# The expert guess of six batches by a sum over the partitions on GpSimd, and two w2 conversions at other hidden blocks

## The chip, the cores and the metric

The kernel runs on one core of a Trainium2 chip. The metric is the device time of one execution in microseconds (us); less is better. Times of the trace count from the start of the profiled span.

## The reference

Two stages: packed attention over 8 batches of 8 heads (576 tokens, 64 wide, 32 packing rows), then a mixture of 8 experts with one expert for each token.

```
p_packed = softmax(p @ k.T / 8) @ v           # per batch and head
out      = softmax(q @ p_packed.T / 8) @ p_packed
x        = out as [4608, 512]                  # 576 tokens of each batch
logits   = normed(x) @ normed(expert_emb).T / tau
expert   = argmax(logits); gate = the softmax's value there
out[t]   = gate[t] * (relu(x[t] @ w1[expert]) @ w2[expert])
```

All tensors are float32.

## The kernel before

The kernel works batch by batch and joins two batches at a time in one hand-made order: while TensorE runs the expert network (`ffn`) of batch b, the attention of batch b+1 is woven in, one piece at each step of `ffn`. `step_att` advances the generator `att_main(b + 1)`, `gates_main` that of the gates; every `yield` is a place where the other generators may put work. The order in which the generators call the engines is the order of each engine's queue, and an engine takes its queue in order.

Since all tokens of a batch are expected to go to one expert, the kernel **guesses** the expert from the packed rows before the tokens are routed. `row_logits` makes 16 logits for each of 128 packed rows on TensorE, `logits_out` (L521) copies them into `x.ppx`, and `guess` sums them over the 128 partitions by a product with ones (`equal`, L629, into PSUM). VectorE takes the largest of eight columns (L635 to L640), and the index is loaded into a register (L644) with which `load_w1` (L933) and `load_w2` (L941) fetch that expert's weights. For batches 2 to 7 GpSimd loads the register and issues these transfers. At the end the number of tokens that went elsewhere is counted, and a slow loop follows if it isn't zero.

`ffn` of a batch has these stages on TensorE: 16 hidden blocks of six products (`hidden`, L1046; f = 0 to 7 for the first half of the tokens, then for the second), each evicted by ScalarE and VectorE (hT, L1050 and L1051); 16 steps' worth of small products L1081; then four output blocks c = 0 to 3 with w2 (L1099). PSUM has three banks for these results (`pf`).

w2 comes as float32 (`w2r`) and is **converted** in eight pieces into a high and a low part (`split_w2`): a cast on ScalarE (L951) and a subtraction on GpSimd (L952). Four of a batch's eight are made during c = 3 of the batch before, four at f = 4 to 7 of the second half of its own hidden blocks.

Of the attention of the next batch these pieces matter here, in the order in which they come: the **key maxima** of both head groups together on VectorE (L343, `quarter_max`, and `whole_max` behind them); the exponentials on ScalarE (L364); `quarter_flip`, which adds the exponentials together by three halvings for each group on GpSimd (L383, into qs) and transposes them on VectorE (L386); the products with the values on TensorE (L396), and right behind them `quarter_totals`, four small products that read qs (L407), and the count of the batch before (L879). Then the logits and the guess, the query scores (L270), the softmax of the queries (L675 on) up to the transposed `x.at`, which `route` multiplies on TensorE (L764).

Of the kernel before, what the change touches and what calls it, by code (L numbers as in the profile page):

```python
# [9 lines left out]
F32 = mybir.dt.float32  # L10
# [4 lines left out]
ALU = mybir.AluOpType  # L15
AX = mybir.AxisListType
# [11 lines left out]
def kernel(  # L28
# [12 lines left out]
    nc = tc.nc  # L41
    B, H, S, D = q.shape
    E, DM, F = w1.shape
    NP = p.shape[2]
    NG = H // HB
# [207 lines left out]
    def idle(n):  # L253
        for _ in range(n):
            yield
# [264 lines left out]
    def logits_out(x, pt):  # L520
        nc.vector.tensor_copy(x.ppx[:, :, 2 * D :], pt[:, : NG * E].rearrange("p (g e) -> p g e", g=NG))  # L521
# [6 lines left out]
    def att1(x, nat, queries=None, other=None):  # L528

        def pack(queries, other):  # L530
            pack_tiles(x)
            if not x.s1:
                quarter_banks(x)
            quarter_scores(x)
            yield
            for g in range(NG):
                quarter_max(x, g)
            yield
            yield from whole_max(x)
            yield from idle(2)  # L540
            for g in range(NG):
                for n in range(HB):
                    quarter_exp(x, g, n)
                    if n:
                        yield
                quarter_flip(x, g)
            yield
            pt = pb.tile([P, 1024], F32, name="pt", tag="pb")
            for g in range(NG):
                quarter_values(x, g, nat(2 * NPR + g), pt[:, g * D : g * D + D])  # L550
            sums = pt[:, NG * D : NG * D + NG * QW // 8]
            quarter_totals(x, sums)
            if other:
                counts(other, pt[:1, 256 : 256 + NC5 * E])
            next(queries)
            yield
            if other:
                counted(other)
            quarter_sums(x, sums.rearrange("p (g k) -> p g k", g=NG))
            for g in range(NG):  # L560
                pair_rows(x, g, pt[:, g * D : g * D + D])
            yield
            next(queries)
            yield
            pu = pc.tile([P, 512], F32, name="pu", tag="pu")
            for g in range(NG):
                pair_turn(x, g, pu)
            nc.vector.tensor_copy(x.T, pu[:, 0 : NG * P])
            yield from idle(2)
            pt = pc.tile([P, 512], F32, name="pu", tag="pu")  # L570
            row_logits(x, pt)
            yield
            logits_out(x, pt)
            next(queries)
            yield

        def pack_slowly():
            pack_tiles(x)
            for g in range(NG):
                pt = pb.tile([P, 1024], F32, name="pt", tag="pb")  # L580
                p1_turn(x, g, pt)
                yield
                p1_evac(x, g, pt)
                key_sum(x, g)
                yield
            pt = pb.tile([P, 1024], F32, name="pt", tag="pb")
            for g in range(NG):
                pack_values(x, g, nat(2 * NPR + g), pt[:, g * D : g * D + D])
            yield
            for g in range(NG):  # L590
                pair_rows(x, g, pt[:, g * D : g * D + D])
            yield
            pu = pc.tile([P, 512], F32, name="pu", tag="pu")
            yield
            for g in range(NG):
                pair_turn(x, g, pu)
            yield
            nc.vector.tensor_copy(x.T, pu[:, 0 : NG * P])
            yield
            pt = pc.tile([P, 512], F32, name="pu", tag="pu")  # L600
            row_logits(x, pt)
            logits_out(x, pt)
            yield

        if x.halves:
            for g in range(NG):
                key_max(x, g)
                yield
                key_exp(x, g)
                yield  # L610
            yield from pack_slowly()
        else:
            asked = queries or all_queries(x, nat)
            yield from pack(asked, other)
            if queries is None:
                drain(asked)


    def guess(x, late=0, engine=mybir.EngineType.Pool, total=None):
        pt = pc.tile([P, 512], F32, name="pu", tag="pu")  # L620
        if total is not None:

            for n in range(NPR):
                nc.tensor.matmul(
                    pt[:1, :E], total[:, n : n + 1], enT[:, n], start=(n == 0), stop=(n == NPR - 1)
                )
        else:
            for g in range(NG):
                nc.tensor.matmul(  # L629
                    pt[:64, :E], equal, x.ppx[:, g, 2 * D :], start=(g == 0), stop=(g == NG - 1)  # L630
                )
        yield
        m8 = sm.tile([1, 8], F32, name="m8", tag="m8", bufs=1)
        idx = sm.tile([1, 8], U32, name="idx", tag="idx", bufs=1)
        nc.vector.max(m8, pt[:1, :E])  # L635
        nc.vector.max_index(idx, m8, pt[:1, :E])
        gi = sm.tile([1, 1], F32, name="gi", tag="gi", bufs=1)
        nc.vector.tensor_copy(gi, idx[:, 0:1])
        x.sel = sm.tile([1, E], F32, name="sel", tag="sel")
        nc.vector.tensor_scalar(  # L640
            out=x.sel, in0=ecol[:1], scalar1=gi, scalar2=None, op0=ALU.is_equal
        )
        yield from idle(late)
        x.e = nc.values_load(  # L644
            idx[0:1, 0:1], engines=[engine], min_val=0, max_val=E - 1,
            skip_runtime_bounds_check_because="an index of the largest of E columns",
        )


    def att2(x, after=None, first=False, b1=False, eng1="vvvvvv"):  # L650
# [344 lines left out]
    def ffn(x, store, late=False, after=None, end=False, between=None):  # L995
# [33 lines left out]
        def hidden(hf, f):  # L1029
            cs = slice(hf * HS, (hf + 1) * HS)  # L1030
            pf = ps.tile([P, 512], F32, name="pf", tag="pf")

            assert not late or hf == 0 or hf in x.lows and x.gs >= NG * (f // 4 + 1)
            if late and hf == 0:
                ops = [
                    (x.g32[f // 4][:, g, f % 4 * P : f % 4 * P + P], x.ats[0][:, g])
                    for g in range(NG)
                ]
            else:
                ops = [  # L1040
                    (x.G[:, a, g, f * P : (f + 1) * P], x.AT[:, m, g, cs])
                    for g in range(NG)
                    for a, m in PASSES
                ]
            for n, (w, r) in enumerate(ops):
                nc.tensor.matmul(pf[:, :HS], w, r, start=(n == 0), stop=(n == len(ops) - 1))  # L1046
            yield
            n = HS if hf == 0 else 512 - HS
            cs = slice(hf * HS, hf * HS + n)
            nc.scalar.activation(hT[:, 0, f, cs], pf[:, :n], AF.Relu)  # L1050
            nc.vector.scalar_tensor_tensor(  # L1051
                out=hT[:, 1, f, cs], in0=pf[:, :n], scalar=0.0,
                in1=hT[:, 0, f, cs].bitcast(F32), op0=ALU.max, op1=ALU.subtract,
            )
            if hf:
                nc.vector.tensor_scalar(
                    out=h4[:, f], in0=pf[:, n:HS], scalar1=0.0, scalar2=None, op0=ALU.max
                )
            if f >= 4 and hf and not late:
                split_w2(x)  # L1060

        if not late and not hasattr(x, "w1g"):
# [98 lines left out]
    def att_main(b):  # L1161
        x = bat[b]
        if b:
            if b > 1:
                quarter_banks(x)
            queries = all_queries(x, nat_main(b)) if b > 1 else None
            yield from att1(x, nat_main(b), queries, bat[b - 1] if b > 1 else None)
            sync = b == 1
            queue = nc.sync if sync else nc.gpsimd
            for n, _ in enumerate(guess(  # L1170
                x, 0 if sync else 2, mybir.EngineType.SP if sync else mybir.EngineType.Pool
            )):
                if n == 1 and queries:
                    next(queries)
                yield
            load_w1(x, x.e, queue=queue)
        flips = keys_main(b + 1) if b else None
        second = att2(x, flips, b == 0, b < 1, ENG1 if b == 1 else "vvvvpv")
        if b:
            if b > 1:  # L1180
                yield
            for _ in range(3 if b == 1 else 2):
                yield next(second)
            load_w2(x, x.e, queue)
            if b == 1:
                yield from idle(3)
        yield from second
        x.soft = True
        if b:
# [470 lines left out]
```

## Time and profile before

| | |
|---|---|
| median of 3 runs | 417.68 us (417.46 to 417.93) |
| the profiled execution | 418.19 us, its span 416.4 us |
| TensorE (PE) busy | 404.1 us, 97% |
| VectorE (DVE) busy | 304.0 us, 73% |
| ScalarE (ACT) busy | 203.0 us, 49% |
| GpSimd (POOL) busy | 159.2 us, 38% |

The span runs from the first to the last instruction; some 1.8 us of the execution lie around it. From about 81 to 370 us the trace repeats one pattern six times, once for each of the batches 1 to 6 whose `ffn` holds the attention of a later one. A start time of a TensorE product is where it enters the array; its end is modelled.

### The profile page before, as it was taken

To read this page: it belongs to the slowest core of one execution; us is meant where nothing else is said; L and a number is where in the kernel's file an instruction comes from. 1 tells how busy PE (TensorE), PEld (TensorE's weight loads), DVE (VectorE), ACT (ScalarE), POOL (GpSimd) and SP (SyncE) were. 2 spreads that over 40 slices of the span, in tenths; PEclk is the share of its full clock that TensorE was granted. 3 is DMA by queue.
4 is the path that set the end of the run, shared out by engine and by line. 5 is a ranking of instruction groups with operands and counts; after the bars stand their busy time and mean duration, and the time that the engine had idled before them with its cause. 6 is when DMAs were issued, how large, how long until landed. Compare 5 with 4: busy or idle time off the path is not lost.

```text
span 416.4 us, 11127 instructions
## 1 busy us (share of the span) xinstructions
PE 404.1 (97%) x4036; PEld 325.9 (78%) x4037; DVE 304.0 (73%) x968; ACT 203.0 (49%) x501; POOL 159.2 (38%) x197
## 2 busy tenths in 40 slices
PE   6899999999999999999999999999999999999993
PEld 3758768797878978798787978689786988779783
DVE  2577696589986889679896889778896798736500
ACT  3577714863256713764147623666038631576110
POOL 2246714536214571236415381146613373142200
PEclk9999999999999999999999999999999999999998
DMA  8999897976989479876999669995899709310021
GB/s 228 308 347 237 222 293 251 237 188 163 283 309 235 135 209 267 304 211 180 260 344 238 158 177 275 327 229 145 230 305 291 195 23 358 111 51 2 20 53 50
DMA packets 42608, 87.93 MB, mean 211 GB/s; under 512 B 11690, under 2 KB 20906, under 8 KB 42546
## 3 DMA queue, kind: packets, MB, share of 16 engines
q1 hardware_dynamic: 35280, 61.44, 53.0%
q0 software_dynamic: 6720, 25.17, 18.9%
q10 hardware_dynamic: 546, 0.54, 0.6%
q8 instruction: 34, 0.56, 0.6%
q14 instruction: 28, 0.23, 0.2%
HBM read 77.68 MB, written 9.44 MB: 209 GB/s over the span
## 4 chain that ended last, share of the span: by engine, by line
PE 92%; DMA 2%; ACT 1%; DVE 1%; POOL 1%; issue 0%; SPq 0%; ACTq 0%; POOLq 0%
PE pf L1099 43%; PE pf L1046 24%; PE pf L1081 7%; PE pt L764 3%; PE pt L976 3%; PE pt L396 2%; PE pt L270 2%; PE pt L331 2%; DMA nat<-in_k 2%; PE pu L764 1%; PE pf L1243 1%; PE pt L1275 1%; PE pt L464 1%; PE pu L501 0%; DMA out<-o 0%
## 5 line engine op out<-in xcount | busy, mean ns | idle before, releaser
L1099 PE MATMUL pf<-w2s,hT 128*128 128x512 f32 (+1 forms) x792 | 181.8, 387 | 0.0
L1099 PEld LDWEIGHTS pf<-w2s,hT 128*128 128x128 f32 x792 | 143.7, 188 | 39.0 <-issue 10.7
L1046 PE MATMUL pf<-AT,G 128*128 128x288 f32 x720 | 102.1, 298 | 0.4 <-DVE hT L1051 0.2
L1046 PEld LDWEIGHTS pf<-AT,G 128*128 128x128 f32 x720 | 97.2, 188 | 4.3 <-issue 1.5
L952 POOL TENSOR_TENSOR w2s<-w2r,w2s 128x512 fp32r<-128x512 f32 x64 | 81.3, 1288 | 41.2 <-ACT w2s L951 35.7
L1051 DVE SCALAR_TENSOR_TENSOR hT<-pf,hT 128x224 fp32r<-128x224 f32 (+1 forms) x128 | 52.3, 414 | 25.9 <-ACT hT L1050 25.5
L1050 ACT ACTIVATE hT<-pf 128x224 fp32r<-128x224 f32 (+1 forms) x128 | 49.3, 386 | 42.8 <-PE pf L1046 40.1
L291 DVE STREAM_TRANSPOSE kt<-nat 128x576 f32<-128x576 f32 x52 | 38.8, 763 | 0.2
L951 ACT CAST w2s<-w2r 128x512 fp32r<-128x512 f32 x64 | 38.9, 621 | 0.0
L1448 ACT ACTIVATE o<-pf,gate 128x512 f32<-128x512 f32 (+1 forms) x41 | 26.0, 636 | 25.8 <-PE pf L1099 15.5
L1081 PE MATMUL pf<-w2r,h 128*64 128x256 f32 x256 | 33.3, 388 | 0.0
L989 DVE TENSOR_TENSOR G<-pt,G 128x1024 fp32r<-128x1024 f32 x14 | 17.1, 1225 | 20.2 <-ACT G L988 20.2
L715 POOL TENSOR_TENSOR AT<-at,AT 128x576 fp32r<-128x576 f32 x7 | 10.0, 1423 | 53.4 <-ACT AT L710 53.4
L914 ACT ACTIVATE lg<-lg 128x40 f32<-128x40 f32 x8 | 1.9, 237 | 52.9 <-DVE lg L910 52.9
L689 ACT ACTIVATE st<-st 128x576 f32<-128x576 f32 (+1 forms) x17 | 11.1, 657 | 33.9 <-DVE st L686 32.7
L383 POOL TENSOR_TENSOR qs<-p 128x320 f32<-128x320 f32 x12 | 10.5, 879 | 40.6 <-ACT p L364 40.6
L777 ACT ACTIVATE scr<-pt 128x512 f32<-128x512 f32 (+2 forms) x33 | 16.7, 508 | 15.2 <-PE pf L764 7.7
L1081 PEld LDWEIGHTS pf<-w2r,h 128*64 128x64 f32 x256 | 19.4, 137 | 4.9 <-PE pu L501 1.0
L871 POOL MEMSET oh<- 64x8 f32 x8 | 0.8, 98 | 53.8 <-DVE oh L867 48.8
L710 ACT CAST AT<-at 128x576 fp32r<-128x576 f32 x15 | 10.1, 674 | 22.7 <-DVE at L704 22.6
L364 ACT ACTIVATE p<-pt,qnm 128x160 f32<-128x160 f32 x48 | 17.8, 398 | 0.0
L941 POOL DMA_DIRECT2D w2r<-in_moe_w x24 | 17.0, 713 | 0.0
(229 smaller groups left out, 510.2 us busy)
## 6 DMA issues: line engine op xcount, KB each, us to landing
nat<-in_q SPq DMA_DIRECT2D x112, 140.0 KB, 3.4
nat<-in_k SPq DMA_DIRECT2D x96, 140.0 KB, 3.9
w1t<-in_moe_w POOLq DMA_DIRECT2D x12, 1024.0 KB, 9.4
w2r<-in_moe_w POOLq DMA_DIRECT2D x24, 512.0 KB, 15.9
out<-o SPq DMA_DIRECT2D x124, 64.0 KB, 2.4
w2r<-in_moe_w SPq DMA_DIRECT2D x8, 512.0 KB, 9.1
vn<-in_v SPq DMA_DIRECT2D x24, 160.0 KB, 3.7
vn<-in_v SPq DMA_DIRECT2D x48, 80.0 KB, 3.6
```

Of the source, the lines that this page charges most:

```text
L291: nc.vector.transpose(kt.rearrange("p (c i) -> p c i", i=32), t)
L364: nc.scalar.activation(x.p1[g][:, n * QW : n * QW + QW], area(x, g)[:, n // 2, n % 2], AF.Exp, bias=x.nm[:, at : at + 1],)
L941: queue.dma_start(t, w2e[:, 2 * i : 2 * i + 2, :])
L951: nc.scalar.copy(t[:, 0], raw)
L952: nc.gpsimd.tensor_tensor(out=t[:, 1], in0=raw, in1=t[:, 0].bitcast(F32), op=ALU.subtract)
L989: nc.vector.tensor_tensor(out=to[1], in0=src, in1=to[0].bitcast(F32), op=ALU.subtract)
L1046: nc.tensor.matmul(pf[:, :HS], w, r, start=(n == 0), stop=(n == len(ops) - 1))
L1050: nc.scalar.activation(hT[:, 0, f, cs], pf[:, :n], AF.Relu)
L1051: nc.vector.scalar_tensor_tensor(out=hT[:, 1, f, cs], in0=pf[:, :n], scalar=0.0, in1=hT[:, 0, f, cs].bitcast(F32), op0=ALU.max, op1=ALU.su ...
L1081: nc.tensor.matmul(pf[64 * hf : 64 * hf + 64, :256], h4[:, f], x.w2r[f // 2][:, f % 2, hf * 256 : hf * 256 + 256], start=(f == 0), stop=(f ...
L1099: nc.tensor.matmul(pf[:, :w], hT[:, a, f, c * P : (c + 1) * P], x.w2s[f][:, m, at : at + w], start=(f == 0 and i == 0), stop=(f == NF - 1 ...
L1448: nc.scalar.activation(o[:, :w], pf[:, :w], AF.Copy, scale=x.gate[:, c : c + 1])
```

## The change

For batches 2 to 7 the two products L629 go. In their place `vote` puts a `tensor_reduce` over the partitions on GpSimd right behind the copy of the logits: 128 partitions of 2 x 8 logits become one row of 2 x 8 in SBUF. `choose_late`, three steps later, adds the two groups on VectorE and takes the largest as before; the register is loaded and w1 fetched one step later still, behind the query scores. Batches 0 and 1 keep their guess by products. And `split_w2` is called at f = 5 and 6 of the first half and f = 4 and 5 of the second half, in place of f = 4 to 7 of the second half.

```diff
@@ att1 @@
             logits_out(x, pt)
+            if other:
+                vote(x)
             next(queries)
@@ guess @@
-        nc.vector.max(m8, pt[:1, :E])
-        nc.vector.max_index(idx, m8, pt[:1, :E])
...
+        x.chosen = choose(x, pt[:1, :E])
+        yield from idle(late)
+        x.e = index_of(x, engine)
+    def vote(x):
+        x.votes = sm.tile([1, NG, E], F32, name="votes", tag="votes", bufs=1)
+        nc.gpsimd.tensor_reduce(x.votes, x.ppx[:, :, 2 * D :], axis=AX.C, op=ALU.add)
+
+    def choose_late(x):
+        t = x.votes[:, 0]
+        nc.vector.tensor_tensor(out=t, in0=t, in1=x.votes[:, 1], op=ALU.add)
+        x.chosen = choose(x, t)
@@ ffn @@
-            if f >= 4 and hf and not late:
+            if f in ((5, 6), (4, 5))[hf] and not late:
                 split_w2(x)
@@ att_main @@
+            else:
                 yield
-            load_w1(x, x.e, queue=queue)
+                next(queries)
+                yield from idle(2)
+                choose_late(x)
+                yield
...
+        elif b:
+            yield next(second)
+            x.e = index_of(x, mybir.EngineType.Pool)
+            load_w1(x, x.e, queue=nc.gpsimd)
+            yield next(second)
+            load_w2(x, x.e, nc.gpsimd)
```

The row numbers of the changed kernel are 7 to 23 higher: L1050 is L1069, L951 and L952 are L970 and L971, L644 is L653.

GpSimd's queue of one period, from the conversions (w2s) ahead of the halvings (qs, of the two groups' exponentials p) to the load of the index, before:

```order
L952 TENSOR_TENSOR w2s<-w2r,w2s 128x512 x4
L383 TENSOR_TENSOR qs<-p_2142 128x320
...
L383 TENSOR_TENSOR qs<-p_2180 128x320
L383 TENSOR_TENSOR qs<-qs 128x4x40
L383 TENSOR_TENSOR qs<-qs 128x2x2x20
L952 TENSOR_TENSOR w2s<-w2r,w2s 128x512 x4
L644 TENSOR_LOAD idx
```

and now, in the same period:

```order
L971 TENSOR_TENSOR w2s<-w2r,w2s 128x512 x6
L383 TENSOR_TENSOR qs<-p_2142 128x320
...
L383 TENSOR_TENSOR qs<-p_2186 128x320
L383 TENSOR_TENSOR qs<-qs 128x4x40
L383 TENSOR_TENSOR qs<-qs 128x2x2x20
L971 TENSOR_TENSOR w2s<-w2r,w2s 128x512 x2
L661 TENSOR_REDUCE votes<-ppx 1x16
L653 TENSOR_LOAD idx
```

The subtractions ahead of the halvings are four of c = 3 of the batch before and now two more; behind the halvings two are left, and the reduction stands between them and the index.

ScalarE's queue at the first half's end (hT are evictions of hidden blocks, p the exponentials of the two groups), before:

```order
L1050 ACTIVATE hT<-pf 128x288 x5
L364 ACTIVATE p_2142<-pt,qnm 128x160 x2
L1050 ACTIVATE hT<-pf 128x288
L364 ACTIVATE p_2142<-pt,qnm 128x160
L1050 ACTIVATE hT<-pf 128x288
...
L1050 ACTIVATE hT<-pf 128x224 x3
L951 CAST w2s<-w2r 128x512
```

and now:

```order
L1069 ACTIVATE hT<-pf 128x288 x5
L364 ACTIVATE p_2142<-pt,qnm 128x160 x2
L1069 ACTIVATE hT<-pf 128x288
L970 CAST w2s<-w2r 128x512
L364 ACTIVATE p_2142<-pt,qnm 128x160
L1069 ACTIVATE hT<-pf 128x288
L970 CAST w2s<-w2r 128x512
```

The two casts stand behind the evictions of f = 5 and 6, ahead of the third and the fourth exponential of the first group.

VectorE's queue at the guess (kt are query transposes, ss, sq, rq and gy the gates of the batch before), before:

```order
L521 COPY ppx<-pu 128x2x8
L291 STREAM_TRANSPOSE kt<-nat 128x576
L635 MAX m_1656<-pu 1x8
L636 MAX_INDEX idx<-m_1656,pu 1x8
L638 CAST gi<-idx 1x1
L640 TENSOR_SCALAR sel<-ecol,gi 1x8
L291 STREAM_TRANSPOSE kt<-nat 128x576
L895 TENSOR_TENSOR ss<-sq 128x2
...
L103 TENSOR_TENSOR rq_t<-rq_h,rq_i 128x5
```

and now:

```order
L521 COPY ppx<-pu 128x2x8
L291 STREAM_TRANSPOSE kt<-nat 128x576 x2
L914 TENSOR_TENSOR ss<-sq 128x2
...
L103 TENSOR_TENSOR rq_t<-rq_h,rq_i 128x5
L665 TENSOR_TENSOR votes<-votes 1x8
L642 MAX m_1673<-votes 1x8
L643 MAX_INDEX idx<-m_1673,votes 1x8
```

The choice now stands behind both transposes and the gates' first operations, and one addition (L665), which waits for GpSimd, is ahead of it.

## Rows read from the trace of the kernel before

**Rows 1.** The page: busy time by engine, and the chain by engine.
```profile
PE 404.1 (97%) x4036; PEld 325.9 (78%) x4037; DVE 304.0 (73%) x968; ACT 203.0 (49%) x501; POOL 159.2 (38%) x197
...
PE 92%; DMA 2%; ACT 1%; DVE 1%; POOL 1%; issue 0%; SPq 0%; ACTq 0%; POOLq 0%
```

**Rows 2.** Stretch of one period: length, busy us (count) by engine, PEclk, DMA.
```profile
core 0: us, PE busy (x) PEld busy (x) DVE busy (x) ACT busy (x) POOL busy (x), PEclk, DMA share, GB/s
...
129.74:177.94 48.20, 48.20 (x498) 39.43 (x498) 39.82 (x122) 23.91 (x60) 19.66 (x25) 1.00 0.82 230
```

**Rows 3.** TensorE's waits, whole span, first and last: total us, times, longest.
```profile
PE pf L1243 <- DMA nat<-in_k: 2.0, 2, 1.1
...
PE pf L1046 <- DVE hT L1051: 0.2, 1, 0.2
```

**Rows 4.** The chain that ended last, around the guess: start us, us, what.
```profile
147.11 0.91 PE pf L1081 x8
148.03 0.12 PE pu L629 x3
148.15 1.83 PE pf L1081 x16
```

**Rows 5.** GpSimd in order of time (start us, us): halvings, conversions; last period's halving.
```profile
137.58 0.88 POOL L383 TENSOR_TENSOR qs<-p 128x320 f32<-128x320 f32 x1 [6.07 <-ACT p L364]
...
139.99 0.88 POOL L383 TENSOR_TENSOR qs<-p 128x320 f32<-128x320 f32 x1 [0.48 <-ACT p L364]
140.95 0.97 POOL L383 TENSOR_TENSOR qs<-qs 128x160 f32<-128x160 f32 x2
...
145.07 3.75 POOL L952 TENSOR_TENSOR w2s<-w2r,w2s 128x512 fp32r<-128x512 f32 x3 [1.16 <-ACT w2s L951]
...
330.35 0.88 POOL L383 TENSOR_TENSOR qs<-p 128x320 f32<-128x320 f32 x1 [6.07 <-ACT p L364]
```

**Rows 6.** ScalarE in order of time: eviction of f = 5, exponential, a cast.
```profile
135.97 0.42 ACT L1050 ACTIVATE hT<-pf 128x288 fp32r<-128x288 f32 x1
136.26 0.42 ACT L364 ACTIVATE p<-pt,qnm 128x160 f32<-128x160 f32 x1
...
144.38 0.61 ACT L951 CAST w2s<-w2r 128x512 fp32r<-128x512 f32 x1
```

**Rows 7.** TensorE in order of time: the first products of L407, two periods.
```profile
142.76 0.21 PE L407 MATMUL pt<-qs,fold 128*32 128x40 f32 x2
...
335.52 0.21 PE L407 MATMUL pt<-qs,fold 128*32 128x40 f32 x2
```

**Rows 8.** VectorE in order of time: logits, choice, gates, transposed x.at.
```profile
147.16 0.17 DVE L521 COPY ppx<-pu 128x16 f32<-128x16 f32 x1
...
148.24 0.16 DVE L635 MAX8 m<-pu 1x8 f32<-1x8 f32 x1
...
149.06 0.78 DVE L291 STREAM_TRANSPOSE kt<-nat 128x576 f32<-128x576 f32 x1
...
150.70 0.17 DVE L103 TENSOR_TENSOR rq_t<-rq_h,rq_i 128x5 f32<-128x5 f32 x1
...
164.89 0.78 DVE L704 STREAM_TRANSPOSE at<-st 128x576 f32<-128x576 f32 x1
```

**Rows 9.** TensorE in order of time: the first product that reads x.at.
```profile
166.27 1.66 PE L764 MATMUL pt<-ppx,at 64*128 64x136 f32 x24
```

**Rows 10.** GpSimd's groups by line and shape: busy us, mean ns, idle before.
```profile
L383 POOL TENSOR_TENSOR qs<-qs 128x160 f32<-128x160 f32 x12 | 6.4, 534 | 0.9
L383 POOL TENSOR_TENSOR qs<-qs 128x80 f32<-128x80 f32 x12 | 4.3, 357 | 0.9
...
L163 POOL TENSOR_SCALAR en_sb<-emb_sb,enrm 8x512 f32<-8x512 f32 x1 | 1.6, 1577 | 2.2 <-DVE enrm L160 2.2
...
L1252 POOL TENSOR_SCALAR wp<-np 128x256 f32<-128x256 f32 x1 | 0.9, 854 | 3.0 <-DMA np<-in_p 3.0
```

**Rows 11.** Loads of w1: issue on GpSimd, us to landing (page), product in the chain.
```profile
149.74 1.52 POOL L933 DMA_DIRECT2D w1t<-in_moe_w  x2 [0.92 <-DVE sel L640]
...
w1t<-in_moe_w POOLq DMA_DIRECT2D x12, 1024.0 KB, 9.4
...
171.75 1.88 PE pt L976 x32
```

More of the change, by code (lines that the diff above doesn't have):

```diff
@@ L616, in att1, with guess @@
                 drain(asked)
-    def guess(x, late=0, engine=mybir.EngineType.Pool, total=None):
+    def guess(x, late, engine, total=None):
         pt = pc.tile([P, 512], F32, name="pu", tag="pu")
@@ L632, in guess, with choose @@
         yield
+        x.chosen = choose(x, pt[:1, :E])
+        yield from idle(late)
+        x.e = index_of(x, engine)
+    def choose(x, votes):
         m8 = sm.tile([1, 8], F32, name="m8", tag="m8", bufs=1)
         idx = sm.tile([1, 8], U32, name="idx", tag="idx", bufs=1)
-        nc.vector.max(m8, pt[:1, :E])
-        nc.vector.max_index(idx, m8, pt[:1, :E])
+        nc.vector.max(m8, votes)
+        nc.vector.max_index(idx, m8, votes)
         gi = sm.tile([1, 1], F32, name="gi", tag="gi", bufs=1)
@@ L642, in guess, with index_of @@
         )
-        yield from idle(late)
-        x.e = nc.values_load(
-            idx[0:1, 0:1], engines=[engine], min_val=0, max_val=E - 1,
+        return idx
+    def index_of(x, engine):
+        return nc.values_load(
+            x.chosen[0:1, 0:1], engines=[engine], min_val=0, max_val=E - 1,
             skip_runtime_bounds_check_because="an index of the largest of E columns",
         )
+    def vote(x):
[5 more added lines that the diff above has]
+        x.chosen = choose(x, t)
     def att2(x, after=None, first=False, b1=False, eng1="vvvvvv"):
@@ L1167, in att_main @@
             yield from att1(x, nat_main(b), queries, bat[b - 1] if b > 1 else None)
[L1168 to L1174, printed above, removed]
+            if b == 1:
+                for _ in guess(x, 0, mybir.EngineType.SP):
+                    yield
+                load_w1(x, x.e)
+            else:
                 yield
-            load_w1(x, x.e, queue=queue)
+                next(queries)
+                yield from idle(2)
+                choose_late(x)
+                yield
         flips = keys_main(b + 1) if b else None
         second = att2(x, flips, b == 0, b < 1, ENG1 if b == 1 else "vvvvpv")
[L1179 to L1182, printed above, removed]
+        if b == 1:
+            for _ in range(3):
                 yield next(second)
-            load_w2(x, x.e, queue)
-            if b == 1:
-                yield from idle(3)
+            load_w2(x, x.e)
+            yield from idle(3)
+        elif b:
[4 more added lines that the diff above has]
+            load_w2(x, x.e, nc.gpsimd)
         yield from second
```

## The prediction

> **What bounds the kernel now.** I read the shares first, then the chain of work that ended last, the stretches batch by batch, and TensorE's own waits. [rows 1] say that TensorE is the bound: 97% of the span busy and 92% of the chain. One batch period is 48.20 us with 48.20 us of TensorE work in it and the clock at 1.00 [rows 2]; TensorE's listed waits run from 2.0 us in total down to 0.2 and all lie in the first 40 us, the opening [rows 3]; asked of 81.5 to 370 us alone, the list is empty. So two kinds of thing move the time: work taken off TensorE, which comes back in full, and a wait that reaches TensorE, which is lost in full. GpSimd is idle half of the period (19.66 us busy of 48.20) [rows 2], but the question is when it is idle, so I then read GpSimd's and ScalarE's instructions one by one around the three places that the change touches. All times below are those of the period from 129.74; the other five repeat it.
>
> **Part 1, the product that goes.** In each of six periods the two float32 products of L629 stand between two runs of L1081. The chain gives them 0.12 us [rows 4]; the 24 products of L1081 around them take 0.91 + 1.83 = 2.74 us, which is the same 0.114 us each on both sides, so nothing waits there and nothing else goes with them. Saved: 6 x 0.12 = 0.7 us.
>
> **Part 2, the two conversions that move.** Each of them is a cast on ScalarE and a subtraction on GpSimd (L952). They go from behind hidden blocks f = 6 and 7 of the second half to behind f = 5 and 6 of the first. What stands behind them there on GpSimd are the six halving additions of L383, which before started at once when their exponentials were there, and what waits for the last of those is TensorE, at L407. So I lay out GpSimd's queue anew. ScalarE evicts f = 5 at 135.97 and takes its next instruction at 136.26 [rows 6]; that is now the first cast, 0.61 us long, to 136.87. GpSimd follows a cast after 0.08 us (144.38 + 0.61 = 144.99 against 145.07 [rows 5, 6]): 136.95. The second cast has one exponential and one eviction of about 0.4 us ahead of it and ends by 138.3 at the latest, about when GpSimd is through with the first subtraction, so the two run as a pair. Three such subtractions take 3.75 us [rows 5], two 2.50: they end at 139.45. Then come both halvings. One took 1.93 us (139.99 to 140.95 + 0.97 = 141.92 [rows 5]); two with 0.05 between them end at about 143.36, where they ended at 141.92 before.
>
> TensorE comes to L407 at 142.76 [rows 7], so before there were 0.84 us to spare, and now it waits about 0.60 us and, with the same 0.08 us from one engine to the next, 0.67. From the start of the first halving to L407 it is 5.18 us here and 335.52 - 330.35 = 5.17 us in the last of the six periods [rows 5, 7], so all six have the same slack. TensorE takes its instructions in order: the count of L879 and the rest of the hidden blocks are queued behind L407, and nothing of it is caught up in an engine that is busy 48.20 of 48.20 us. ScalarE's two casts also push back its evictions (hT, L1050) and so VectorE's; a bank that comes back late could make TensorE wait a little before L407 already. This is not a second cost: GpSimd's chain hangs on ScalarE's exponentials and not on TensorE there, so such a wait is part of the same 0.67. Bounds: 0.60 without any hand-over time, 0.85 if the second cast ends at 138.3 and every hand-over costs 0.08.
>
> At the place that the conversions leave, f = 6 and 7 of the second half, they hid behind TensorE. Their going frees GpSimd earlier for the vote, and moves nothing on TensorE: a gain of 0.
>
> **Part 3, the vote.** GpSimd's reduction over the partitions (128 x 16 into 1 x 16) is in no row. It can start when the logits are copied, 147.16 + 0.17 = 147.33 [rows 8], and GpSimd is free by then, since the two conversions left in the second half end near 147.1. VectorE now comes to the choice later: behind one more query transpose and three operations of the gates, with the four operations of the choice (148.24 to 149.06, 0.82 us) no longer ahead of them, so at 150.70 + 0.17 - 0.82 = 150.05 [rows 8]. A reduction of up to 2.65 us is free. Behind the choice VectorE has an unbroken run up to the transposed x.at, ready at 164.89 + 0.78 = 165.67 [rows 8], for which TensorE asks at 166.27 [rows 9]: 0.60 us of slack, less the 0.12 by which TensorE is earlier there and about 0.2 for the one operation added (L665). That leaves some 0.28 us, so the reduction costs nothing up to about 2.9 us, and beyond that each microsecond is a microsecond of TensorE in each of six batches.
>
> What may it cost? GpSimd's time goes by columns: 160 and 80 columns take 534 and 357 ns, which is 2.2 ns a column on 0.18 us, and 8 partitions cost as much a column as 128 (1577 ns for 512, 854 ns for 256) [rows 10]. If the partitions run side by side, 16 columns cost 0.22 us; if the 128 x 16 values are taken one after the other, 2048 x 2.2 ns + 0.18 = 4.7 us. I take a value under 2.9, as an estimate, because all rows of this engine show partitions that run side by side, and keep 4.7 for the range. [...]
>
> The loads of w1 and w2 are issued by GpSimd behind the index. The index is ready some 2 us later than before, so w1's transfers start near 152 in place of 149.74; at 9.4 us to landing they are there by 162, and the product with w1 comes at 171.75 [rows 11]. They cost 0.
>
> **Sum.** Per period -0.12 + 0.67 = +0.55 us; six periods +3.3 us (2.9 to 4.4 by the bounds). The profiled execution, 418.19 us with a span of 416.4, becomes 421.5 with a span of 419.7; the median of the runs shown, 417.68, becomes 421.0 (+0.8%).
>
> **Rivals.** *A, the reduction is long.* GpSimd works its way through the partitions, the choice holds VectorE, and TensorE waits at L764 for x.at. For it: a crossing of partitions is the one thing that no GpSimd row here does. Against it: the room of 2.9 us is most of the way from 0.22 to 4.7. It decides from 2.9 us on; at 4.7 us it is 6 x 1.8 = 10.8 us more, 432; a typical case of it, 3.7 us, gives 426.
>
> *B, no wait at L407, so not slower.* The wait is a difference of 0.60 us out of 6.4 us of GpSimd work in a row; if GpSimd runs a filled queue of these eight instructions a tenth faster than the rows show them, or the first cast comes 0.6 us earlier, the halvings end before 142.76 and only the saved product is left: 417.68 - 0.7 = 417.0, within 0.2%. For it: the halvings were never seen back to back with conversions. Against it: three conversions in a row took 1.25 us each, so a filled queue gains little.
>
> *C, both.* TensorE stops at neither place, and the freed evictions of the second half give back a little more: 416.5. Nothing in the rows of TensorE's waits speaks for it.
>
> **How the numbers follow.** The forecast has 0.64, A 0.21, B 0.10, C 0.05. The range runs from 418.8 to 429: it holds the forecast with its bounds (420.6 to 422.1), a wait at L407 that is half as long, and most of A, and leaves out B, C and the top of A (together under 0.2). A measurement of this kernel can tell about 0.2% (0.8 us) from no change. Faster by more than that: C and a little of B, 0.07. Within it: the rest of B, and a wait of about 0.2 us, 0.12. Slower: 0.81.
>
> **What would show it.** Right: GpSimd's first halving starts near 139.5 by this period's clock, straight behind the moved subtractions and not idle before it; a gap of TensorE ahead of L407 that ends with L383; a period of about 48.75 us; no gap of TensorE ahead of L764. A period of 48.08 with the halvings ended before L407 would be B. A reduction longer than 2.9 us on GpSimd with VectorE idle ahead of L665, and a gap at L764, would be A. The forecast is wrong at its root if the period grows and the gap lies in neither place.

## Result, and the profile of the changed kernel

| | before | changed |
|---|---|---|
| median of 4 runs | 417.57 us (417.34 to 417.93) | 421.06 us (420.81 to 423.65) |
| the profiled execution, its span | 418.19 us, 416.4 us | 421.17 us, 419.5 us |

The changed kernel is slower by 0.9%: the ratio, changed over before, is 1.0092, 95% interval 1.0071 to 1.0113. Forecast were 421.0 us and, for the profiled execution, 421.5 us. Each experiment below has its ratio against the kernel before as timed beside it (medians 417.57 to 417.97 us). In these timings one run of the kernel before took 1009.54 us and one of a version below, with one conversion moved, 1006.99 us, for a reason that nothing on record shows; the ratios leave both out.

The page of the changed kernel, its busy times and the chain that ended last by engine [rows 1]; behind them, from the chain in order of time (start us, us, what), the start of the first and of the sixth batch period:

```profile
PE 407.7 (97%) x4012; PEld 323.3 (77%) x4013; DVE 304.2 (73%) x974; ACT 201.1 (48%) x501; POOL 170.9 (41%) x203
...
PE 85%; ACT 6%; DMA 4%; DVE 3%; issue 1%; SPq 0%; ACTq 0%
```
```profile
82.22 1.19 PE pt L331 x40
...
325.96 1.25 PE pt L331 x42
```

TensorE is still 97% busy, but its share of the chain fell from 92% to 85%: some of the chain now runs through ScalarE and VectorE. The period, read as a fifth of the way from the first to the sixth row, is (325.96 - 82.22) / 5 = 48.75 us. Read the same way it was (323.27 - 82.33) / 5 = 48.19 before. I compare periods below rather than totals, since the start of the first one varies by itself, from 81.4 to 83.1 us over the kernels of this study.

TensorE's waits between 81 and 372 us, where the list of before was empty (line waited for: us in total, times, longest):

```profile
PE pf L1065 <- DVE h L1075: 1.1, 6, 0.2
```

One wait in each of six periods, at a **hidden block**, not at L407. To see what it costs, look at TensorE's weight loads (PEld) in order of time (start us, us, in brackets the idle time before and what ended it; L1065 is the hidden block, L396 the product with the values):

```profile
139.59 0.83 PEld L1065 LDWEIGHTS pf<-AT,G 128*128 128x128 f32 x6 [0.23 <-DVE hT L1070]
140.81 1.63 PEld L1065 LDWEIGHTS pf<-AT,G 128*128 128x128 f32 x12 [0.39 <-PE pf L1065]
142.61 1.29 PEld L396 LDWEIGHTS pt<-vn,p1T 128*32 128x32 f32 x80 [0.16 <-issue]
143.90 0.16 PEld L407 LDWEIGHTS pt<-qs,fold 128*32 128x32 f32 x8
```

The fourth eviction of this half stands at 135.55 in place of 135.11, so this period's clock runs 0.44 us ahead of that of before, and L396 comes at 142.17 in its time. Before it was 141.58, behind one unbroken row of loads (138.34, 3.07 us, 22 of them). So 0.59 us are lost ahead of L396, in two gaps of 0.23 and 0.39. L407 comes at 143.46 in the time of before, against 142.76 [rows 7]: 0.70 lost by there. Only the last 0.1 can be a wait for the halvings. GpSimd in order of time shows that they end just then [rows 5]:

```profile
137.42 2.55 POOL L971 TENSOR_TENSOR w2s<-w2r,w2s 128x512 fp32r<-128x512 f32 x2 [5.18 <-ACT w2s L970]
139.93 0.88 POOL L383 TENSOR_TENSOR qs<-p 128x320 f32<-128x320 f32 x1
...
142.88 0.97 POOL L383 TENSOR_TENSOR qs<-qs 128x160 f32<-128x160 f32 x2
...
148.56 2.01 POOL L661 CROSS_LANE_REDUCE votes<-ppx 128x16 f32<-128x16 f32 x1 [1.08 <-DVE ppx L521]
```

The two moved subtractions run as a pair, the halvings follow without a pause and end at 143.85, and TensorE's L407 comes at 143.90. Why the hidden block waits is seen on ScalarE [rows 6]; first the changed kernel from the first moved cast on, then the last two of these evictions before:

```profile
136.70 0.64 ACT L970 CAST w2s<-w2r 128x512 fp32r<-128x512 f32 x1
137.21 0.42 ACT L364 ACTIVATE p<-pt,qnm 128x160 f32<-128x160 f32 x1
137.50 0.44 ACT L1069 ACTIVATE hT<-pf 128x288 fp32r<-128x288 f32 x1
137.79 0.66 ACT L970 CAST w2s<-w2r 128x512 fp32r<-128x512 f32 x1
...
138.59 0.46 ACT L1069 ACTIVATE hT<-pf 128x288 fp32r<-128x288 f32 x1
```
```profile
136.81 0.41 ACT L1050 ACTIVATE hT<-pf 128x288 fp32r<-128x288 f32 x1
...
137.60 0.41 ACT L1050 ACTIVATE hT<-pf 128x288 fp32r<-128x288 f32 x1
```

Each cast puts 0.51 us between an eviction and the next exponential. The evictions, 0.79 us apart there before, are 1.09 apart behind each cast; in the clock of before the third of them comes at 138.15 in place of 137.60, 0.55 late. VectorE finishes each eviction behind ScalarE, the three banks come back late, and TensorE stands: VectorE's part of that third eviction (L1070) runs from 139.08 to 139.54, and the weight loads go on at 139.59.

The vote takes 2.01 us and ends at 150.57. VectorE asks for it at 150.88, straight behind the first operations of the gates, and TensorE meets no wait at L783 (L764 of before):

```profile
150.88 0.15 DVE L665 TENSOR_TENSOR votes<-votes 1x8 f32<-1x8 f32 x1
...
166.27 0.78 DVE L723 STREAM_TRANSPOSE at<-st 128x576 f32<-128x576 f32 x1
```

### The profile page after: what moved, and what is told of

Read it like the earlier page. It is cut to its first block, busy times and chain, and to the rows that moved or that the text cites. A ratio compares the mean times of both kernels' runs of the same rounds, so it can differ in the third digit from the quotient of the medians.

```text
span 419.5 us, 11079 instructions
## 1 busy us (share of the span) xinstructions
PE 407.7 (97%) x4012; PEld 323.3 (77%) x4013; DVE 304.2 (73%) x974; ACT 201.1 (48%) x501; POOL 170.9 (41%) x203
## 4 chain that ended last, share of the span: by engine, by line
PE 85%; ACT 6%; DMA 4%; DVE 3%; issue 1%; SPq 0%; ACTq 0%
PE pf L1118 42%; PE pf L1065 18%; PE pf L1100 7%; DMA nat<-in_k 3%; PE pt L783 3%; PE pt L995 3%; ACT hT L1069 2%; PE pt L396 2%; PE pt L270 2%; PE pt L331 2%; ACT p L364 2%; ACT w2s L970 1%; PE pu L783 1%; DVE hT L1070 1%; DVE p1T L386 1%; PE pf L1266 1%
## 5 line engine op out<-in xcount | busy, mean ns | idle before, releaser
L971 POOL TENSOR_TENSOR w2s<-w2r,w2s 128x512 fp32r<-128x512 f32 x64 | 81.7, 1290 | 67.4 <-ACT w2s L970 66.4
L1065 PE MATMUL pf<-AT,G 128*128 128x288 f32 x720 | 104.4, 299 | 1.3 <-DVE h L1075 1.1
L1065 PEld LDWEIGHTS pf<-AT,G 128*128 128x128 f32 x720 | 97.3, 188 | 7.6 <-PE pf L1065 2.7
L1069 ACT ACTIVATE hT<-pf 128x224 fp32r<-128x224 f32 (+1 forms) x128 | 50.5, 395 | 45.9 <-PE pf L1065 45.1
L1070 DVE SCALAR_TENSOR_TENSOR hT<-pf,hT 128x224 fp32r<-128x224 f32 (+1 forms) x128 | 52.4, 415 | 26.3 <-ACT hT L1069 25.6
L970 ACT CAST w2s<-w2r 128x512 fp32r<-128x512 f32 x64 | 39.4, 629 | 0.0
L1100 PE MATMUL pf<-w2r,h 128*64 128x256 f32 x256 | 32.0, 386 | 0.0
L1100 PEld LDWEIGHTS pf<-w2r,h 128*64 128x64 f32 x256 | 16.9, 137 | 8.4 <-PE pu L501 1.0
L364 ACT ACTIVATE p<-pt,qnm 128x160 f32<-128x160 f32 x48 | 19.4, 440 | 0.0
L783 PEld LDWEIGHTS pt<-ppx,at 64*128 64x128 f32 x208 | 12.9, 187 | 3.8 <-issue 2.5
```

The source lines that it names most:

```text
L364: nc.scalar.activation(x.p1[g][:, n * QW : n * QW + QW], area(x, g)[:, n // 2, n % 2], AF.Exp, bias=x.nm[:, at : at + 1],)
L783: nc.tensor.matmul(to, x.at[at, g, tokens], x.ppx[at, g], start=True, stop=True, tile_position=(64 * half, column),)
L970: nc.scalar.copy(t[:, 0], raw)
L971: nc.gpsimd.tensor_tensor(out=t[:, 1], in0=raw, in1=t[:, 0].bitcast(F32), op=ALU.subtract)
L1070: nc.vector.scalar_tensor_tensor(out=hT[:, 1, f, cs], in0=pf[:, :n], scalar=0.0, in1=hT[:, 0, f, cs].bitcast(F32), op0=ALU.max, op1=ALU.su ...
L1100: nc.tensor.matmul(pf[64 * hf : 64 * hf + 64, :256], h4[:, f], x.w2r[f // 2][:, f % 2, hf * 256 : hf * 256 + 256], start=(f == 0), stop=(f ...
```

## Experiments

### One half of the change at a time

The moved conversions with the product kept, made from the kernel before:

```diff
-            if f >= 4 and hf and not late:
+            if f in ((5, 6), (4, 5))[hf] and not late:
                 split_w2(x)
```

> The kernel before with the two conversions moved as in the change, and the guess by the product kept. Theory: the whole loss is the conversions', 0.7 us a period: 417.6 + 6 x 0.7 = 421.8 us, a little above the changed kernel (421.06) by the product that is kept. Rival, the vote has a share in the loss: below 421.

Measured: 421.93 us, ratio 1.0106 (1.0085 to 1.0127), period 48.88, the same wait at the hidden block. The moves cost 48.88 - 48.19 = 0.69 us a period, which is the whole loss, and the changed kernel, with the vote for the product, is 48.88 - 48.75 = 0.13 us a period shorter. That looks like the 0.12 of the forecast, but it is the net of two things. The first weight loads of the next batch (L331), where one period meets the next, here and then in the changed kernel:

```profile
179.19 0.94 PEld L331 LDWEIGHTS pt<-kt,pw 64*32 64x32 f32 x64 [0.16 <-issue]
```
```profile
179.69 0.96 PEld L331 LDWEIGHTS pt<-kt,pw 64*32 64x32 f32 x64 [0.32 <-PE pf L1065]
```

With the product the stretch up to L331 is the same at every such place. With the vote it is longer by 0.06 to 0.15 us at four of the five (0.09 on the mean), and at these four L331 starts 0.115 us behind the end of VectorE's L320, as it does in the next kernel, where the list of waits names L320. Counted without that gap the period is 0.22 us shorter. So the product that went took 0.22, and 0.09 of it is lost again, because VectorE is later there.

The vote with the conversions left where they were, made from the changed kernel:

```diff
-            if f in ((5, 6), (4, 5))[hf] and not late:
+            if f >= 4 and hf and not late:
```

> The change with the conversions left at f = 4 to 7 of the second half, so that the vote stands behind four of them on GpSimd. Theory: they end at 148.82 by the clock of the period of before, the vote takes 2.0 us (2.00 to 2.01 in the changed kernel) and ends at 150.85, VectorE asks at 150.05 and waits 0.8 us; the run up to x.at has 0.1 to 0.28 us of slack, so TensorE waits 0.5 to 0.7 us at L764, less 0.12: 420 to 421 us. Rival, the slack is larger than that or VectorE makes it up: 416.9 us.

Measured: 422.66 us, ratio 1.0122 (1.01 to 1.0144), period 49.25. That is 1.17 more than the 48.08 that the saved product alone would leave, and more than expected. TensorE's list of waits, GpSimd around the vote, VectorE, and TensorE's weight loads:

```profile
PE pt L331 <- DVE pt L320: 3.9, 5, 0.8
```
```profile
145.82 3.75 POOL L971 TENSOR_TENSOR w2s<-w2r,w2s 128x512 fp32r<-128x512 f32 x3 [1.16 <-ACT w2s L970]
149.53 2.01 POOL L661 CROSS_LANE_REDUCE votes<-ppx 128x16 f32<-128x16 f32 x1
```
```profile
149.44 0.14 DVE L914 TENSOR_TENSOR ss<-sq 128x2 f32<-128x2 f32 x1
...
150.14 1.43 DVE L92 TENSOR_SCALAR rq_i<-ss 128x5 int32<-128x5 int32 x1
150.22 1.36 DVE L98 TENSOR_SCALAR rq_h<-ss 128x5 f32<-128x5 f32 x1
...
151.69 0.15 DVE L665 TENSOR_TENSOR votes<-votes 1x8 f32<-1x8 f32 x1
...
167.07 0.78 DVE L723 STREAM_TRANSPOSE at<-st 128x576 f32<-128x576 f32 x1
```
```profile
173.54 0.18 PEld L995 LDWEIGHTS pt<-w1t,T 64*32 64x32 f32 x16 [0.98 <-ACT scr L796]
...
180.50 0.96 PEld L331 LDWEIGHTS pt<-kt,pw 64*32 64x32 f32 x64 [0.96 <-PE pf L1065]
```

Three of the four conversions stand straight ahead of the vote, which starts at 149.53 and ends at 151.54. Two small operations of the gates, 0.17 us each elsewhere, begin beside the reduction, last 1.4 us, and end with it (151.57 and 151.58). L665 then comes at 151.69. But this hold is not what costs the time. In the changed kernel L665 comes 0.36 us behind the start of L92, which would be 150.50 here; the row of votes wasn't written before 151.54, so L665 would have waited some 1.1 us in any case (an estimate from these rows), and the hold adds about 0.1. What costs is that the vote ends late behind four conversions. The expectation had this wait as 0.8 us and counted on slack behind it; VectorE's run is late by all of 1.2 us, and so is the period.

Little of the gap is at L783, though x.at comes 1.4 us later in the clock of before (164.89 there [rows 8]): the products of L783 that read the first half of x.at start at 166.78, while the second half is made from 167.07 to 167.85, and the stretch is longer by at most 0.24 us in the six periods. Most of the delay comes out later, at the product with w1 (L995) and at the next batch's L331.

### Which of two waits

In the changed kernel the late bank and the late halvings stand at the same place. Two kernels have one of them each. Both divide `split_w2` into its cast and its subtraction:

```diff
+    def cast_w2(x):
+        f = len(x.w2s)
...
+        nc.scalar.copy(t[:, 0], x.w2r[f // 2][:, f % 2, :])
+        x.w2s.append(t)
+        x.cast = getattr(x, "cast", []) + [f]
+
+    def rest_w2(x):
+        f = x.cast.pop(0)
+        t = x.w2s[f]
```

The first has the casts where the change puts them, and both subtractions behind the halvings (`at` is the pair of half and f):

```diff
-            if f in ((5, 6), (4, 5))[hf] and not late:
-                split_w2(x)
...
+                for _ in range(((0, 5), (0, 6)).count(at)):
+                    cast_w2(x)
+                for _ in range(((1, 3), (1, 3)).count(at)):
+                    rest_w2(x)
+                for _ in range(((1, 4), (1, 5)).count(at)):
+                    split_w2(x)
```

> The changed kernel with the two moved casts left on ScalarE at f = 5 and 6 of the first half, but their two subtractions on GpSimd put behind the halvings (all four then stand there). Theory, two places: in the changed kernel the time is lost at two places that overlap, a PSUM bank that comes back late because the casts push the evictions back (0.59 us lost by the start of L396), and the halvings (0.1 us more at L407). Then this kernel keeps the bank wait and loses about 0.55 us a period less 0.12 saved: 420.0 us, halvings on GpSimd ended 0.5 us or more before L407. Rival, halvings only (the place named in the prediction): without the subtractions ahead of them nothing waits, 416.9 us. Rival, banks only: 420.6 us, as the changed kernel less 0.

Measured: 423.01 us, ratio 1.0125 (1.0095 to 1.0155), period 48.89. Its waits, its weight loads, one row of VectorE and one of GpSimd:

```profile
PE pf L1075 <- DVE h L1085: 1.1, 6, 0.2
PE pu L512 <- DVE T L568: 0.3, 1, 0.3
```
```profile
140.38 0.84 PEld L1075 LDWEIGHTS pf<-AT,G 128*128 128x128 f32 x6 [0.20 <-DVE hT L1080]
141.60 1.63 PEld L1075 LDWEIGHTS pf<-AT,G 128*128 128x128 f32 x12 [0.38 <-PE pf L1075]
```
```profile
145.32 0.73 DVE L416 TENSOR_SCALAR qr<-qr 128x2 f32<-128x2 f32 x1
```
```profile
143.49 5.03 POOL L982 TENSOR_TENSOR w2s<-w2r,w2s 128x512 fp32r<-128x512 f32 x4
```

The two bank gaps are those of the changed kernel (0.20 and 0.38 for 0.23 and 0.39), with the halvings ended at 143.53, a microsecond ahead of L407 at 144.52. So the casts alone are enough for the 0.59 us ahead of L396, and the theory that the halvings alone cause the loss has fallen. The total misses the expectation by 3 us. About half of that lies in the six periods (48.89, where 0.55 lost and 0.12 saved would make 48.62 of the 48.19 of before): behind the bank gaps TensorE's weight loads stand 0.52 us at L512, ahead of which VectorE's L416 lasts 0.73 us (0.52 in the changed kernel) beside four subtractions in a row. That L416 is what makes L568, and so L512, late fits the order of VectorE's queue but was not tested, and the other half of the miss stays open.

The second has the casts early, at f = 0 and 1 of the first half, and both subtractions between the halvings of the two groups, `(1, 0)` twice for `rest_w2` (the other two conversions stay at f = 4 and 5 of the second half):

```diff
+                for _ in range(((0, 0), (0, 1)).count(at)):
+                    cast_w2(x)
+                for _ in range(((1, 0), (1, 0)).count(at)):
+                    rest_w2(x)
```

> The changed kernel with the two casts at f = 0 and 1 of the first half, where ScalarE is idle, and their two subtractions between the halvings of the first and of the second group on GpSimd. Theory, two places: no bank wait, but the halvings end at 139.51 + 2.50 + 1.93 + 0.08 = 144.02 by the clock of the period of before, against 142.76 for L407: 1.3 us of wait a period, less 0.12, times six: 424.7 us. Rival, banks only: the evictions are on time, so nothing is lost: 416.9 us.

Measured: 423.8 us, ratio 1.0142 (1.0117 to 1.0167), period 49.22. Waits, GpSimd, weight loads:

```profile
PE pt L407 <- POOL qs L383: 5.4, 6, 0.9
```
```profile
141.26 2.54 POOL L982 TENSOR_TENSOR w2s<-w2r,w2s 128x512 fp32r<-128x512 f32 x2
...
144.71 0.95 POOL L383 TENSOR_TENSOR qs<-qs 128x160 f32<-128x160 f32 x2
```
```profile
145.71 0.16 PEld L407 LDWEIGHTS pt<-qs,fold 128*32 128x32 f32 x8 [1.04 <-POOL qs L383]
```

No bank gap, and TensorE stands at L407 until the halvings end at 145.66. So the wait that the prediction laid out exists too, and alone it costs in full: 1.14 us a period. In the changed kernel the two delays run at the same time, and the later one sets the loss.

### Places that were thought free

If only L407 and the banks count, both conversions at f = 0 and 1 of the first half, ahead of the exponentials, should cost nothing.

```diff
-            if f in ((5, 6), (4, 5))[hf] and not late:
-                split_w2(x)
...
+                for _ in range(((0, 0), (0, 1), (1, 4), (1, 5)).count(at)):
+                    split_w2(x)
```

> The changed kernel with the two whole conversions at f = 0 and 1 of the first half in place of f = 5 and 6. Both theories on the conversions: GpSimd has them done by about 135 us of that period, the halvings start where they did before, the casts fall where ScalarE waits for TensorE; only the saved product is left, 417.57 - 0.7 = 416.9 us, period 48.08 us. Rival, the vote costs too: VectorE's run up to x.at ended only 0.1 us before TensorE asked for it in the changed kernel, so a little may be lost at L764 (L783 in the changed numbering) and the time is that of the kernel before, 417.6 us. Rival, the key maxima: casts that stand beside the joined key maxima delay the evictions there and cost 0.3 us a period or more: 418.7 us.

Measured: 422.67 us, ratio 1.0132 (1.0107 to 1.0157), period 49.09: a full miss. VectorE, GpSimd and the weight loads there:

```profile
133.77 1.17 DVE L352 TENSOR_TENSOR qlow<-qm,qlow 64x8 f32<-64x8 f32 x1
```
```profile
133.63 1.29 POOL L982 TENSOR_TENSOR w2s<-w2r,w2s 128x512 fp32r<-128x512 f32 x1 [0.66 <-ACT w2s L974]
```
```profile
135.68 6.64 PEld L1075 LDWEIGHTS pf<-AT,G 128*128 128x128 f32 x48 [0.94 <-DVE qnm L356]
```

An operation of 64 x 8 in the joined key maxima, 0.16 us before, takes 1.17 in all six periods. It begins 0.14 us behind a subtraction on GpSimd and ends with it (134.94 against 134.92). The rest of the maxima and VectorE's next eviction of a hidden block stand behind it in VectorE's queue, and TensorE's loads stand 0.94 us, by the list until L356, one of the last steps of the maxima, ends. The third rival had named the right neighbour, the key maxima, but had it that the casts delay the evictions. So this place is not free: beside the conversions there stands a chain of small operations on VectorE which TensorE waits for. One reading that fits these rows is that GpSimd's subtraction holds L352 until it ends; this run alone does not decide it.

If GpSimd's subtraction holds L352, the one that falls on L352 has only to be brought forward. Both conversions at f = 0:

```diff
+                for _ in range(((0, 0), (0, 0), (1, 4), (1, 5)).count(at)):
+                    split_w2(x)
```

> The run named early with both conversions at f = 0 of the first half, not one each at f = 0 and 1. In that run VectorE's L352, a tensor_tensor with two inputs in SBUF that takes 0.16 us elsewhere, took 1.17 us and ended as GpSimd's second subtraction ended, and TensorE lost 1.0 us a period behind it. Theory, the operation was shut out by GpSimd's subtraction: with both casts at f = 0 the second subtraction ends about 0.9 us earlier, at 134.0 to 134.1 by the clock of the period of before, where L352 comes at 133.9, so at most 0.2 us of it is left: 417.0 to 418.0 us, L352 under 0.4 us. Rival, the early casts hold up ScalarE's evictions or the subtractions slow VectorE as such: the loss stays, 422 us or more.

Measured: 419.39 us, ratio 1.0033 (1.002 to 1.0047), period 48.46.

```profile
133.32 0.67 DVE L351 COPY qlow<-qm 64x8 f32<-64x8 f32 x1
134.03 0.16 DVE L352 TENSOR_TENSOR qlow<-qm,qlow 64x8 f32<-64x8 f32 x1
```
```profile
127.48 6.49 POOL L982 TENSOR_TENSOR w2s<-w2r,w2s 128x512 fp32r<-128x512 f32 x5 [0.71 <-ACT w2s L974]
```

L352 is back at 0.16, and of the loss of 1.01 us (49.09 - 48.08) 0.38 is left. It is the copy ahead of it, 0.17 us long before, that now is held, 0.50 us here and 0.30 in the first period (0.47 us in the chain there), here until the last of five subtractions ends (133.99 against 133.97). The direction was right, the size not: I had not counted the copy.

### What the vote has left

The reduction twice, on the kernel with both conversions at f = 0 and 1:

```diff
-        nc.gpsimd.tensor_reduce(x.votes, x.ppx[:, :, 2 * D :], axis=AX.C, op=ALU.add)
+        for _ in range(2):
+            nc.gpsimd.tensor_reduce(x.votes, x.ppx[:, :, 2 * D :], axis=AX.C, op=ALU.add)
```

> The conversions at f = 0 and 1 of the first half (as in the run named early) and the vote made twice, one behind the other, into the same row. Theory: the second ends at 147.33 + 4.1 = 151.4 against 150.05 at which VectorE asks: 1.35 us of wait, less 0.1 to 0.28 us of slack, 1.1 to 1.25 us a period lost at L764, less 0.12: 416.9 + 6 x 1.15 = 423.8 us. Rival, no one waits for the vote: 416.9 us.

Measured: 432.71 us, ratio 1.0357 (1.0336 to 1.0378), period 50.82. Against its own base (422.67 and 49.09) that is 10.0 us and 1.73 us a period, where 6.9 us were expected.

```profile
154.67 0.15 DVE L666 TENSOR_TENSOR votes<-votes 1x8 f32<-1x8 f32 x1 [1.72 <-POOL votes L662]
```
```profile
PE pt L331 <- DVE pt L320: 3.9, 5, 0.8
PE pt L784 <- DVE at L724: 2.1, 4, 0.5
```

All of VectorE's 1.72 us of waiting is lost on TensorE: against its base 0.40 to 0.82 us a period at L784, where the products of the second half of x.at wait, about 0.3 at the product with w1 and 0.7 to 0.8 at L331. So VectorE's run behind the choice has no slack to give, and rival A was a true mechanism; it begins where the reduction is longer than about 2.01 + 0.31 = 2.3 us (in the changed kernel VectorE comes 0.31 us behind its end), not at 2.9.

### One conversion moved

A cast pushes ScalarE back by 0.51 us, and GpSimd had 0.84 us to spare at L407; one moved conversion, at f = 5, should fit both. First with the casts and subtractions divided as above, one moved and three left, with the vote:

```diff
+                for _ in range(((0, 5), (1, 4), (1, 5), (1, 6)).count(at)):
+                    split_w2(x)
```

> The changed kernel with only one conversion at f = 5 of the first half and three at f = 4 to 6 of the second half. Theory, both waits with their thresholds: one cast pushes the evictions back by 0.55 us for one block only, ScalarE is on time again at f = 7; the halvings end at 136.95 + 1.25 + 1.93 + 0.05 + 1.93 = 142.1 us against 142.76; nothing waits: 416.9 us. The vote starts at about 147.6 and ends at 149.6, before VectorE asks at 150.05. Rival, each moved conversion costs its share: half of the changed kernel's loss, 0.3 us a period less, 419.2 us.

Measured: 416.73 us, ratio 0.9984 (0.9966 to 1.0002), period 48.11, no wait in TensorE's list between 81 and 372 us.

Then as a pair in more runs, without and with the vote. On the kernel before, with the product:

```diff
-            if f >= 4 and hf and not late:
+            if (hf, f) in ((0, 5), (1, 4), (1, 5), (1, 6)) and not late:
```

> The kernel before with one conversion at f = 5 of the first half and three at f = 4 to 6 of the second half, and the guess by the product kept: the twin of the next run. Theory: nothing waits at either place, so this is the time of the kernel before within 0.2%, period 48.19 us, and 0.12 us a period more than the twin with the vote. Rival, the place freed behind f = 7 gives something of its own (its cast no longer stands between evictions): below the kernel before by more than 0.2%.

Measured: 417.72 us, ratio 0.9997 (0.9981 to 1.0012), period 48.25. On the changed kernel, the same order with the vote:

```diff
-            if f in ((5, 6), (4, 5))[hf] and not late:
+            if f in ((5,), (4, 5, 6))[hf] and not late:
```

> The changed kernel with only one conversion at f = 5 of the first half and three at f = 4 to 6 of the second (the same instructions in the same order as in the run named one moved, timed again with more rounds). Theory: only the saved product is left, 0.12 us a period, 0.7 us in all: 0.9983 of the kernel before, period 48.08 to 48.11 us. Rival: the gain of the earlier run was chance of the opening, and the ratio is 1.

Measured: 417.15 us, ratio 0.9982 (0.9969 to 0.9996), period 48.12. GpSimd and the weight loads:

```profile
136.76 1.29 POOL L971 TENSOR_TENSOR w2s<-w2r,w2s 128x512 fp32r<-128x512 f32 x1 [5.17 <-ACT w2s L970]
...
140.97 0.97 POOL L383 TENSOR_TENSOR qs<-qs 128x160 f32<-128x160 f32 x2
...
147.41 2.01 POOL L661 CROSS_LANE_REDUCE votes<-ppx 128x16 f32<-128x16 f32 x1
```
```profile
137.86 3.41 PEld L1065 LDWEIGHTS pf<-AT,G 128*128 128x128 f32 x24
141.43 1.24 PEld L396 LDWEIGHTS pt<-vn,p1T 128*32 128x32 f32 x78 [0.16 <-issue]
```

The row of hidden blocks is unbroken again, the halvings end at 141.94, 0.6 us ahead of L407 at 142.56, and with one conversion fewer ahead of it than in the kernel with the vote alone, the reduction starts at 147.41 and ends at 149.42, before VectorE comes to L665, at about 149.6 (an estimate: from 142.56 the 4.45 us of before from the first weight loads of L407 to the logits' copy, 142.71 to 147.16, and the 2.57 us of the changed kernel from there to L665). What is left is the same net as in the first pair: 48.25 - 48.12 = 0.13 us a period, 0.22 for the product that went less 0.09 at L331. This version beats both kernels, the one before by some 0.7 us: the interval of its first timing takes in no change, that of the second only just leaves it out.

## Why the prediction was right, and where its steps were not

**The sum held.** Forecast was a period of 48.75 us, measured 48.75; 421.0 us, measured 421.06. The wait of 0.67 came as 0.70, for the queue that the prediction had laid out, and that is why it was right. That the rest agrees to the hundredth is luck.

**Part 1, the product, was mis-sized.** 0.12 was read from the chain. In each of the two pairs of kernels that differ by the product and the vote the period is 0.22 us shorter once the gap at L331 is taken out. The forecast's 0.12 is close to the net 0.13 only because the vote, counted as free, gives 0.09 of the 0.22 back.

**Part 2, GpSimd's queue, held to the tenth.** In the clock of before the first moved subtraction starts at 136.98 (136.95 forecast), the first halving at 139.49 (139.45), the last ends at 143.41 (143.36), and L407 comes at 143.46 (142.76 + 0.67 = 143.43). The kernel with the subtractions alone shows that this queue holds TensorE.

**The place of the gap was wrong.** The prediction named a gap ahead of L407 that ends with L383. In the changed kernel 0.59 of the 0.70 us are lost before that, at banks that ScalarE's casts bring back late; L407 adds 0.1 (0.10 us more from L396 to the next hidden block than with the casts alone). The text allowed for such a wait as "a little", inside the same 0.67. That it is no second cost is right, since both run at once, but its size was never worked out, though ScalarE's rows had it: two casts of 0.51 us are 1.02 us more on an engine whose evictions are due every 0.79. The kernel with the casts alone shows that the bank gap would be there without the halvings. The two delays happened to be nearly equal, and the longer of them, which sets the time of L407, was the one that the prediction had worked out. That the other was not longer is luck.

**Part 3, the vote.** 2.0 us lies within the bounds of 0.22 and 4.7, and VectorE does not wait for it: it asks 2.57 us behind the start of the logits' copy (148.31 to 150.88), where 2.89 was forecast (147.16 to 150.05), so 2.3 us were free and not 2.65. (Seven operations of the gates stand ahead of the choice there, not three; the forecast's time was read behind the seventh all the same.) The prediction's estimate, under 2.9 us, held with 2.01 in the trace. Three other readings were wrong. The vote was to cost nothing up to 2.9 us, and at 2.0 it cost 0.09 us a period at L331. The slack of 0.28 us was looked for at L764, but the first 16 of the 24 products there read only the first half of x.at, so that place has more; L331 has none, and the doubled reduction lost all of its 1.72 us at L764's place, the product with w1 and L331 together. And the place that the conversions leave was counted as a gain of 0. The kernel with the vote alone shows that one conversion must leave it: with four there, the vote ends some 1.1 us behind VectorE's turn, and the period is 1.17 us longer than the 48.08 of the saved product alone.

**The rivals.** B fell, since the halvings end at 143.41 in the clock of before, not before 142.76, and the banks were late as well; with one conversion moved it is what happens. A did not decide at 2.0 us. C was seen in no kernel: with one conversion moved and the product kept, the period is 48.25 us, no shorter than the 48.19 of before.

## What to carry to other kernels

When work moves to another place, lay out the queue of every engine that it runs on, not only of the one with the longest instruction: here the 0.51 us casts on ScalarE made TensorE lose 0.59 us a period, nearly what the 1.29 us subtractions on GpSimd made of it, 0.70. Where two delays meet at the same stretch, the longer one counts, and mending one of them shows little; with half of the work moved both were gone. A list of TensorE's waits that names 0.2 us can stand for a loss of 0.6: compare the start of the next fixed product with that of the kernel before. And a gain that agrees with its forecast can be a larger gain less a loss that no list names, as the 0.13 us here.

## What the runs showed of the hardware

- The sum over 128 partitions of 16 columns on GpSimd takes 2.00 to 2.02 us, and two in a row 4.08; this engine's additions of 80 columns take 0.36 us [rows 10].
- Three kinds of small VectorE operations lasted longer beside a GpSimd instruction and ended within 0.04 us of its end: 64 x 8 with two inputs 1.17 us in place of 0.16 (L352, both conversions at f = 0 and 1) and a copy of 64 x 8 0.67 in place of 0.17 (L351, both at f = 0), each beside a subtraction; `tensor_scalar` of 128 x 5 1.43 and 1.36 in place of 0.17 (L92 and L98, the vote alone), beside the reduction.
- Not all are held: in the changed kernel L914, L918 and L920, `tensor_tensor` operations of 128 x 2, 128 x 1 and 64 x 1 with two inputs, begin 1.29 to 1.70 us into the reduction of 2.01 us and run their usual 0.12, 0.15 and 0.16 us. Which difference lets them pass was not tried.
